# A finer source order, blank matmuls and another load order at the beginning of a fused attention and MoE kernel

## The chip, the cores and the metric

The kernel runs on one core of one Trainium2 chip, as one program. The metric is the device time of that core in microseconds; each run is one execution, and what counts is the median of the runs.

## What is computed

The reference chains three parts. `p` holds 32 pack vectors per head; the attention first packs keys and values into 32 rows per head, and the queries then attend to those rows. The result goes through a mixture of four experts, all of them used, weighted by `domain_probs`, and last through a two-layer map with `h - tanh(h)` between its layers.

```python
q, k, v: (4, 8, 576, 64)   p: (4, 8, 32, 64)      # batch, heads, tokens, head size
def sm_attn(qq, kk, vv):
    s = scale * np.matmul(qq, kk.transpose(0, 1, 3, 2))
    s = s - np.max(s, axis=-1, keepdims=True)
    a = np.exp(s)
    a = a / (np.sum(a, axis=-1, keepdims=True) + 1e-09)
    return np.matmul(a, vv)
p_packed = sm_attn(p, k, v)
out = sm_attn(q, p_packed, p_packed)              # 2304 tokens x 512
for e in range(4):                                # w1: 512 x 1024, w2: 1024 x 512
    h = np.maximum(x @ w1[e], 0.0)
    out += p[:, e:e + 1] * (h @ w2[e])
h = x @ w_in; g = h - np.tanh(h); return g @ w_out
```

## The kernel before

The large products are made of pairs of numbers: a float is split into a high part (`...h`, a copy of 512 to 1024 columns on ScalarE) and a low part (`...l`, the difference on VectorE), and three matmuls stand for one. The tokens are worked in two halves `p` of two batches each, 9 tiles of 128 tokens per half. The experts are worked as 8 chunks `c` of 512 hidden columns.

The program is written as strings of tokens; a letter names a stage, the digits its arguments, and `run` calls them in order.

- **S** `pack_scores`: 4 score matmuls `sc` into a two-bank PSUM tile (pool `ps2`, two such tiles in all, which `tp`, `wps` and `hps` share), `mx` and `nm` on VectorE, the exponential `a` on ScalarE with its sum `ss`, and the norm (`ss`, `rs`, `a`) on VectorE. The digits are the half, then 0 to 3: batch 0 groups 0 and 1, batch 1 groups 0 and 1.
- **T** `pack_T`: five transposes `tp` of `a`, copied out as `a1t` (ScalarE) and `a1e` (VectorE). **P** `pack_pv`: 20 small matmuls `pv` of v with them, copied into `ppbd` by one instruction of ScalarE and one of VectorE.
- **Q** `q_scores`: the q scores `qsc` of two token tiles against `ppbd`, in a one-bank PSUM tile (pool `ps1`, four tiles, which `pv`, `qtp` and `yps` share), and their softmax: `qmx` and the difference on VectorE, the exponential on ScalarE, sum, add, reciprocal and product (`qsm`, `a`) on VectorE. Q04 is one token tile, half as wide. **X** `q_T`: four transposes `qtp`, split into `a2h` and `a2l`.
- **W** `pack_w1`: since x is a2 times packed rows, `ppbd` is multiplied into w1 instead (`wps`, 16 small matmuls, split into `wph` on ScalarE and `wpl` on VectorE). One W per chunk and batch; it needs all of that batch's `P`.
- **u** `up`: the hidden layer of 256 or 320 tokens, 24 matmuls `hps` in two halves, each half in its own `ps2` tile, split into `hu` or `hm`. The last digit is the range of tokens: 0 needs X00, 1 needs X01 and X02 as well and writes the tiles that 2 shares. **d** `down`: 12 matmuls `yps` of one token tile, taken to `x2` by ScalarE in chunk 0, by VectorE later.
- **a** loads half a w1 or w2 chunk; **b** splits w2 (`w2h` on ScalarE, `w2l` on GpSimd in chunk 0, on VectorE later). **K**, **V**, **L** load k, v and q of one batch, in up to four transfers each. **I** and **Z** set up buffers, **n** makes the expert weights from `domain_probs`. `_` is one step of decoding the last map's weights, which goes on in the background.

All loads are issued by SP and share one queue with at most eight in flight. The first ones stand in source order (`manual_schedule` on SP). START_A and START_B, which hold chunk 0 of the experts and all of the attention, are handed to a scheduler that sets the order on each engine from its own estimates; so neighbours in the strings are interleaved there. From chunk 1 on TensorE's order is that of the source. TensorE executes its instructions in order, as every engine does, so a matmul whose operand is late holds all that stand behind it.

Of the kernel before, what the change touches and what calls it, by code (L numbers as in the profile page):

```python
# [8 lines left out]
F32 = mybir.dt.float32  # L9
# [13 lines left out]
R = -11.571460516996891  # L23
# [32 lines left out]
def kernel(  # L56
# [100 lines left out]
    def pack_scores(b, g):  # L157
        sc = ps2.tile([128, 2, 512], F32, tag="p2", name="sc")
        for jj in range(2):
            j = 2 * g + jj  # L160
            for h in range(2):
# [53 lines left out]
    def q_scores(p, t0):  # L215
# [27 lines left out]
        nc.scalar.activation(out=a2[:, 0:n], in_=a2[:, 0:n], func=ACTF.Exp, scale=0.125)  # L243
        sm = small.tile([128, 16, 1], F32, tag="qsm", name="qsm")
# [10 lines left out]
    def q_T(p, t0):  # L255
# [201 lines left out]

    STAGES = {
# [234 lines left out]
```

## Time and profile before

| what | value |
|---|---|
| median of 3 runs (lowest to highest) | 1109.77 us (1108.91 to 1109.89) |
| the profiled execution, its span | 1110.56 us, 1108.8 us |
| TensorE busy | 1090.1 us, 98% of the span, 6420 instructions |
| VectorE busy | 713.5 us, 64%, 967 instructions |
| ScalarE busy | 466.4 us, 42%, 653 instructions |
| GpSimd busy | 7.3 us, 1%, 11 instructions |
| mean granted TensorE clock | 0.996 |
| read and written in HBM | 69.51 MB, 26.21 MB |

The span is what the trace covers, from the first instruction to the last; the 1.76 us that the profiled execution took beyond it lie around it. "Busy" counts the time in which an engine had an instruction under way; matmuls are pipelined, so that it is no measure of TensorE at its peak. In the rows below, an engine's instructions of one kind that follow each other are one row with their count, and the time is that of all of them. Lines are those of the kernel before; `PE` is TensorE, `DVE` VectorE, `ACT` ScalarE, `POOL` GpSimd. What stands behind "<-" is what the idle time ended with: an engine's instruction or a load.

### The profile page before, as it was taken

What the parts mean: (1) busy time and instruction counts of PE and PEld (TensorE: products, weight loads), DVE (VectorE), ACT (ScalarE), POOL (GpSimd) and SP (SyncE); (2) the same over time, 40 slices, a digit from 0 to 9 for tenths busy, and PEclk for the clock granted to TensorE, in tenths of its full rate; (3) what the DMA queues carried; (4) which work ended last, traced back from release to release, by engine and by line L of the source; (5) the groups of instructions that cost most, each with busy time, mean ns of one, the idle gap of its engine ahead of it and who ended that gap; (6) DMA issues with size and microseconds to landing.
All of it is one profiled execution on the core that took longest, in us unless ns stands there. A gap on an engine that the chain in (4) does not pass through costs nothing.

```text
span 1108.8 us, 15316 instructions
## 1 busy us (share of the span) xinstructions
PE 1090.1 (98%) x6420; PEld 911.1 (82%) x6420; DVE 713.5 (64%) x967; ACT 466.4 (42%) x653; POOL 7.3 (1%) x11
## 2 busy tenths in 40 slices
PE   7799999999999999999999999999999999999998
PEld 5587888898888888889888888888888888888887
DVE  4735456766676675676676434487666767777775
ACT  3433433232332332332333112466657656656463
POOL 0100000000000000000000000000000000000000
PEclk9899999999999999999999999999999999999999
DMA  9731013233233241342231042201011262202102
GB/s 332 238 89 39 29 48 115 77 96 114 95 114 95 77 147 63 95 134 77 87 123 58 20 152 77 76 1 38 2 37 39 85 220 95 76 1 76 64 13 76
DMA packets 33668, 96.70 MB, mean 87 GB/s; under 512 B 3776, under 2 KB 3776, under 8 KB 33600
## 3 DMA queue, kind: packets, MB, share of 16 engines
q1 hardware_dynamic: 33600, 95.73, 25.2%
q8 instruction: 50, 0.82, 0.3%
q14 instruction: 18, 0.15, 0.0%
HBM read 69.51 MB, written 26.21 MB: 86 GB/s over the span
## 4 chain that ended last, share of the span: by engine, by line
PE 98%; DVE 1%; ACT 0%; DMA 0%; issue 0%; DVEq 0%; SPq 0%; ACTq 0%
PE yps L391 36%; PE hps L365 18%; PE ops L605 18%; PE h3ps L549 18%; PE wps L340 3%; PE pv L205 1%; PE sc L162 1%; PE qsc L227 1%; PE xps L426 1%; PE qtp L262 1%; PE tp L188 0%; DMA kt<-in_kT_dram 0%; ACT a L173 0%; DVE wpl L347 0%; DVE mx L168 0%
## 5 line engine op out<-in xcount | busy, mean ns | idle before, releaser
L391 PE MATMUL yps<-w2h,hm 128*128 128x512 f32 x640 | 208.4, 394 | 0.0
L549 PE MATMUL h3ps<-xh,ws 128*128 128x512 f32 (+1 forms) x640 | 187.3, 369 | 0.0
L605 PE MATMUL ops<-ws,gh 128*128 128x512 f32 x576 | 178.4, 396 | 0.0
L391 PE MATMUL yps<-w2h,hu 128*128 128x512 f32 x512 | 166.5, 391 | 0.0
L402 DVE SCALAR_TENSOR_TENSOR x<-yps,pn,x 128x512 f32<-128x512 f32 x126 | 94.6, 750 | 100.6 <-PE yps L391 98.0
L365 PE MATMUL hps<-a2h,wph 128*128 128x256 f32 (+1 forms) x512 | 151.8, 297 | 2.4 <-ACT a L173 1.5
L365 PE MATMUL hps<-a2h,wpl 128*128 128x256 f32 (+1 forms) x512 | 151.8, 297 | 0.0
L365 PE MATMUL hps<-a2l,wph 128*128 128x256 f32 (+1 forms) x512 | 151.7, 296 | 0.0
L391 PEld LDWEIGHTS yps<-w2h,hm 128*128 128x128 f32 x640 | 120.1, 188 | 36.3 <-issue 12.6
L549 PEld LDWEIGHTS h3ps<-xh,ws 128*128 128x128 f32 x640 | 116.5, 188 | 20.5
L605 PEld LDWEIGHTS ops<-ws,gh 128*128 128x128 f32 x576 | 107.7, 189 | 24.0 <-ACT gh L584 0.2
L391 PE MATMUL yps<-w2l,hm 128*128 128x512 f32 x320 | 125.2, 391 | 0.0
L549 PE MATMUL h3ps<-xl,ws 128*128 128x512 f32 (+1 forms) x320 | 117.9, 368 | 0.0
L391 PEld LDWEIGHTS yps<-w2h,hu 128*128 128x128 f32 x512 | 96.2, 188 | 19.2
L374 ACT ACTIVATE hu<-hps 128x512 fp32r<-128x512 f32 x64 | 38.2, 598 | 173.1 <-PE hps L365 173.0
L605 PE MATMUL ops<-ws,gl 128*128 128x512 f32 x288 | 110.8, 395 | 0.0
L374 ACT ACTIVATE hm<-hps 128x640 fp32r<-128x640 f32 x64 | 45.1, 704 | 136.1 <-PE hps L365 136.1
L365 PEld LDWEIGHTS hps<-a2h,wph 128*128 128x128 f32 x512 | 97.1, 190 | 6.0 <-ACT a L173 1.7
L391 PE MATMUL yps<-w2l,hu 128*128 128x512 f32 x256 | 100.1, 391 | 0.0
L365 PEld LDWEIGHTS hps<-a2l,wph 128*128 128x128 f32 x512 | 97.2, 190 | 2.3
L365 PEld LDWEIGHTS hps<-a2h,wpl 128*128 128x128 f32 x512 | 97.1, 190 | 0.5 <-issue 0.4
L375 DVE SCALAR_TENSOR_TENSOR hm<-hps,hm 128x640 fp32r<-128x640 f32 x64 | 52.7, 823 | 61.1 <-ACT hm L374 61.1
(90 smaller groups left out, 1392.1 us busy)
## 6 DMA issues: line engine op xcount, KB each, us to landing
w1f<-in_w_dram SPq DMA_DIRECT2D x16, 512.0 KB, 4.9
st<-in_w_dram SPq DMA_DIRECT2D x16, 512.0 KB, 3.8
f<-in_win_dram SPq DMA_DIRECT2D x16, 512.0 KB, 3.5
f<-in_wout_dram SPq DMA_DIRECT2D x16, 512.0 KB, 3.5
win<-fo SPq DMA_DIRECT2D x16, 512.0 KB, 2.6
wout<-fo SPq DMA_DIRECT2D x16, 512.0 KB, 2.6
ws<-win SPq DMA_DIRECT2D x16, 512.0 KB, 4.6
ws<-wout SPq DMA_DIRECT2D x16, 512.0 KB, 4.7
```

Of the source, the lines that this page charges most:

```text
L162: nc.tensor.matmul(out=sc[64 * jj:64 * jj + 64, h, 0:288], lhsT=pbd[:, 4 * b + j, :], rhs=kv_k[b][j][:, 288 * h:288 * h + 288],)
L205: nc.tensor.matmul(out=pv[64 * h:64 * h + 64, jj, :], lhsT=kv_v[b][c][0:n, 128 * j + 64 * h:128 * j + 64 * h + 64], rhs=a1t[:, c, k0:k0 + ...
L227: nc.tensor.matmul(out=sc[r - r0:r - r0 + 64, 256 * i:256 * i + 256].rearrange("p (r j k) -> p r j k", r=2, j=4)[:, :, j, :], lhsT=qs[2 * ...
L262: nc.tensor.transpose(tp[:, g, i, :], a2[:, c0:c0 + 128], ident)
L340: nc.tensor.matmul(out=ps[32 * j:32 * j + 32, r, :], lhsT=ppbd[p][d, bi, j, 32 * r:32 * r + 32], rhs=w1f[c, j // 2][d, j % 2, :],)
L365: nc.tensor.matmul(out=ps[:, ff, 0:n], lhsT=a[c, p, bi][:, g, c0:c0 + 128], rhs=x[p][:, g, t0:t0 + n], start=(k == 0), stop=(k == 5),)
L374: last[1] = nc.scalar.activation(out=hi[:, :, d], in_=ps[:, :, 0:n], func=ACTF.Relu).ins
L375: last[0] = nc.vector.scalar_tensor_tensor(out=lo[:, :, d], in0=ps[:, :, 0:n], scalar=0.0, in1=f(hi[:, :, d]), op0=ALU.max, op1=ALU.subtra ...
L391: nc.tensor.matmul(out=ps, lhsT=a[:, ff, o:o + 128], rhs=w[c, fp][:, ff], start=(k == 0), stop=(k == 11),)
L402: last[0] = nc.vector.scalar_tensor_tensor(out=x2[tt], in0=ps, scalar=pn[:, tt, e:e + 1], in1=x2[tt], op0=ALU.mult, op1=ALU.add,).ins
L549: nc.tensor.matmul(out=ps[:, ff, 0:n], lhsT=w[:, wl, kd, :], rhs=x[:, kd, :], start=(k == 0), stop=(k == 11),)
L605: nc.tensor.matmul(out=ops[u][t], lhsT=a[ff][:, d], rhs=w[:, wl], start=(i == 0 and ff == 0 and k == 0), stop=(i == 3 and ff == 1 and k == 2),
```

## The change

Five things change, all of them in the attention and chunk 0.

1. S is cut into M (matmuls), E (max and exponential) and N (norm), and Q's norm becomes R, so that the source can put other work between. S stays as the three in a row.
2. T takes two one-bank tiles of `ps1` (`tp`, `te`) in place of one two-bank tile of `ps2`, and `a1e` is copied by ScalarE.
3. `fill` issues blank matmuls: 128x128, float, of a tile of zeros with itself, into a `ps1` tile `warm` that nothing reads. There are 26: 7 at the start, 5 before T00, 5 before M02, 5 before X00 and 4 before T02. While it lives, three `ps1` tiles are left for the rest.
4. TensorE, SP, VectorE and ScalarE follow the source in START_A and START_M, SP also in START_L, and TensorE to the end of the experts. In between, VectorE and ScalarE are the scheduler's from START_L on. The first `up` (u000) stands before M03, T03, P03, W001 and Q02, and the steps d000 and d001 before u001. `q_T` records its last instructions in `last`, and the expert weights (n) are issued after `last[0]`.
5. The first loads come as pst, k0, v0, domain_probs, q0, k1, w1 (2), v1, w2 (2), q1; before it was pst, k0, k1, v0, v1, w1 (2), domain_probs, q0, q1, w2 (2). Chunk 1's first pair of w2 loads (a110, a111), which SP issued after V3 and from 50.08 us on, now stands ahead of K2, K3, V2 and V3 there. Batch 1's tiles come from the pools of the later ones; `p_att` has 12 buffers in place of 18.

```diff
-START_A = (
-    "S00 S01 S02 T00 S03 T01 P00 T02 P01 T03 P02 P03 Z0 a100 a101 "
-)
+START_A = "f7 M00 E00 M01 E01 N00 N01 f5 T00 T01 P00 P01 Q00 Q01 f5 M02 f5 R00 E02 N02 X00 "
+
+START_M = "W000 f4 T02 R01 u000 b00 M03 X01 E03 P02 b01 N03 T03 P03 W001 Q02 "
+
+START_L = "R02 K2 I1 n K3 V2 V3 d000 Q04 R04 Q03 R03 d001 X02 S10 S11 "
 
 START_B = (
-    "W000 Q00 Q01 X00 K2 W001 I1 n Q02 X01 S10 u000 V2 b00 b01 K3 V3 X02 S11 Q04 Q03 u001 d000 X03 S12 "
-    "T10 u002 S13 X04 d001 T11 d002 P10 d003 T12 P11 P12 T13 L2 u003 d005 d004 P13 L3 Z1 Q10 Q11 W010 "
-    "W011 d006 Q12 X10 d007 d008 u010 a010 Q13 X11 d010 X12 a011 u011 Q14 X13 d011 u012 a110 "
+    "u001 X04 X03 d002 T10 S12 u002 S13 T11 P10 d003 T12 P11 d004 T13 P12 L2 u003 d005 P13 L3 Z1 d006 Q10 R10 "
+    "Q11 R11 W010 W011 d007 Q12 R12 X10 d008 u010 a010 Q13 R13 X11 d010 X12 a011 u011 Q14 R14 X13 d011 u012 a110 "
     "X14 d013 u013 a111 b10 d012 W100 d015 W101 d016 d014 d017 b11 d018 u100 "
 )
...
-    def pack_scores(b, g):
-        sc = ps2.tile([128, 2, 512], F32, tag="p2", name="sc")
+    scs, sms = {}, {}
+
+    def pack_mm(b, g):
+        sc = scs[b, g] = ps2.tile([128, 2, 512], F32, tag="p2", name="sc")
...
+
+    def pack_exp(b, g):
+        sc = scs.pop((b, g))
...
+        a1s[b, g] = a1, ss
+
+    def pack_norm(b, g):
+        a1, ss = a1s[b, g]
         nc.vector.tensor_scalar(out=ss, in0=ss, scalar1=1e-9, scalar2=None, op0=ALU.add)
         rs = small.tile([128, 1], F32, tag="rs", name="rs")
         nc.vector.reciprocal(out=rs, in_=ss)
         nc.vector.tensor_scalar(out=a1, in0=a1, scalar1=rs, scalar2=None, op0=ALU.mult)
         a1s[b, g] = a1
 
+    def pack_scores(b, g):
+        pack_mm(b, g)
+        pack_exp(b, g)
+        pack_norm(b, g)
+
     def pack_T(b, g):
         a1 = a1s.pop((b, g))
-        tp = ps2.tile([128, 2, 4, 128], F32, tag="p2", name="tp")
-        for c in range(5):
-            n = 128 if c < 4 else 64
-            nc.tensor.transpose(tp[0:n, c // 4, c % 4, :], a1[:, 128 * c:128 * c + n], ident)
+        tp = ps1.tile([128, 4, 128], F32, tag="p1", name="tp")
+        te = ps1.tile([128, 128], F32, tag="p1", name="te")
+        for c in range(4):
+            nc.tensor.transpose(tp[:, c, :], a1[:, 128 * c:128 * c + 128], ident)
+        nc.tensor.transpose(te[0:64, :], a1[:, 512:576], ident)
         a1t = att_tile(b, [128, 4, 128], "a1t")
         a1e = att_tile(b, [128, 128], "a1e")
-        nc.scalar.activation(out=a1t, in_=tp[:, 0], func=ACTF.Copy)
-        nc.vector.tensor_copy(out=a1e[0:64], in_=tp[0:64, 1, 0])
+        nc.scalar.activation(out=a1t, in_=tp, func=ACTF.Copy)
+        nc.scalar.activation(out=a1e[0:64], in_=te[0:64], func=ACTF.Copy)
...
+        a2s[p, t0] = a2, a23, G
+
+    def q_norm(p, t0):
+        a2, a23, G = a2s[p, t0]
...
-        nc.scalar.activation(out=a2h[p][:, :, d], in_=src, func=ACTF.Copy)
-        nc.vector.tensor_tensor(
+        last[1] = nc.scalar.activation(out=a2h[p][:, :, d], in_=src, func=ACTF.Copy).ins
+        last[0] = nc.vector.tensor_tensor(
             out=a2l[p][:, :, d], in0=src, in1=f(a2h[p][:, :, d]), op=ALU.subtract
-        )
+        ).ins
...
+    def fill(n):
+        for i in range(n):
+            nc.tensor.matmul(out=warm[:, i % 4, :], lhsT=blank, rhs=blank)
+
+    def late_norm():
+        with tc.issue_after(last[0]):
+            norm_probs()
...
+    blank = const.tile([128, 128], F32, name="blank")
+    nc.vector.memset(blank, 0.0)
+    warm = ps1.tile([128, 4, 128], F32, tag="p1", name="warm")
     pst = p_att.tile([128, 4 * B, 32], F32, tag="a", name="pst")
     with tc.manual_schedule(engines={mybir.EngineType.SP}):
         nc.sync.dma_start(out=pst, in_=pT)
         load_k(0)
+        load_v(0)
+        nc.sync.dma_start(out=pn, in_=dp)
+        load_q(0)
         load_k(1)
-        load_v(0)
-        load_v(1)
         stage(0, 0, 0)
         stage(0, 0, 1)
-        nc.sync.dma_start(out=pn, in_=dp)
-        load_q(0)
+        load_v(1)
+        stage(1, 0, 0)
+        stage(1, 0, 1)
         load_q(1)
...
-    run(START_A)
+    rest = {mybir.EngineType.SP, mybir.EngineType.DVE, mybir.EngineType.Activation}
+    pe_order = ExitStack()
+    pe_order.enter_context(tc.manual_schedule(engines={mybir.EngineType.PE}))
+    begin = ExitStack()
+    begin.enter_context(tc.manual_schedule(engines=rest))
+    run("Z0 " + START_A)
     att_stack.close()
     p_wp = pool("wp", 2, pa)
+    p_hm = pool("hm", 4, pa)
     p_hu = pool("hu", 8, pa)
-    p_hm = pool("hm", 4, pa)
-    p_w2 = pool("w2", 8, pa)
+    run(START_M)
+    begin.close()
+    with tc.manual_schedule(engines={mybir.EngineType.SP}):
+        run(START_L)
     run(START_B)
-    with tc.manual_schedule(engines={mybir.EngineType.PE}):
-        for c in range(1, NCH):
-            w = {"c": c, "e": c + 1}
-            nxt = c + 1 < NCH
-            run(EVEN % w)
-            run(ODD % w if nxt else LAST)
+    for c in range(1, NCH):
+        w = {"c": c, "e": c + 1}
+        nxt = c + 1 < NCH
+        run(EVEN % w)
+        run(ODD % w if nxt else LAST)
+    pe_order.close()
```

What this does to the engines' order shows at three places. In the rows below, each engine's instructions stand in order; an xN counts neighbours of a kind, a number behind `a_` tells buffers apart, and what stands left of "<-" is written.

TensorE in after, from M03 (`sc`) over X01, P02, T03 (`tp`, `te`), P03, W001 and Q02 to d000:

```order
L166 MATMUL sc<-kt,pbd 64x288 x4
L283 MATMUL qtp<-ident,a_384 128x128 x4
L222 MATMUL pv<-a1t,vt 64x32 x8
L222 MATMUL pv<-a1e,vt 64x32 x2
L222 MATMUL pv<-a1t,vt 64x32 x8
L204 MATMUL tp<-ident,a_522 128x128 x4
L205 MATMUL te<-ident,a_522 64x128
L361 MATMUL wps<-w1f,ppbd 32x512 x8
L244 MATMUL qsc<-ppbd,qt 64x2x32 x16
L412 MATMUL yps<-w2h,hu 128x512
```

TensorE in before, from the `wps` of W000 over P02, P03, the rest of W000, Q00 with Q01, W001, X00, Q02 and X01 to the first `up`:

```order
L340 MATMUL wps<-w1f,ppbd 32x512 x2
L205 MATMUL pv<-a1t,vt 64x32 x8
L205 MATMUL pv<-a1e,vt 64x32 x2
L340 MATMUL wps<-w1f,ppbd 32x512 x6
L227 MATMUL qsc<-ppbd,qt 64x2x32 x32
L340 MATMUL wps<-w1f,ppbd 32x512 x8
L262 MATMUL qtp<-ident,a_462 128x128 x4
L227 MATMUL qsc<-ppbd,qt 64x2x32 x16
L262 MATMUL qtp<-ident,a_489 128x128 x4
L162 MATMUL sc<-kt,pbd 64x288 x2
L365 MATMUL hps<-a2h,wph 128x256
```

What moved: W000's and W001's `wps` stood ahead of X00 and around Q00; W001 now stands behind P03, the transposes of T03 between P02 and P03, and the first `up` ahead of all these rows, with the blanks.

TensorE in after, from the end of d001 over X02, S10 and S11 to the first half of u001:

```order
L412 MATMUL yps<-w2l,hu 128x512
L412 MATMUL yps<-w2h,hu 128x512
L283 MATMUL qtp<-ident,a_622 128x128 x4
L166 MATMUL sc<-kt,pbd 64x288 x8
L386 MATMUL hps<-a2h,wph 128x320
L386 MATMUL hps<-a2l,wph 128x320
L386 MATMUL hps<-a2h,wpl 128x320
```

TensorE in before at u001, from the end of u000 over the second half of S11, X02 and Q04 with Q03, with the first `yps` of d000 after the first matmul of u001:

```order
L365 MATMUL hps<-a2h,wpl 128x256
L162 MATMUL sc<-kt,pbd 64x288 x4
L262 MATMUL qtp<-ident,a_551 128x128 x4
L227 MATMUL qsc<-ppbd,qt 64x2x32 x24
L365 MATMUL hps<-a2h,wph 128x320
L391 MATMUL yps<-w2h,hu 128x512
L365 MATMUL hps<-a2l,wph 128x320
L365 MATMUL hps<-a2h,wpl 128x320
```

What moved: d000 and d001, and both scores, now stand whole ahead of u001, where d000 stood among its matmuls.

VectorE in after, the norms of Q04 (`a_694`) and Q03 (`a_721`), then X02's `a2l` and the maxima of S10 and S11:

```order
L257 TENSOR_TENSOR a_721<-qsc,qmx 128x512
L266 TENSOR_REDUCE qsm<-a_694 128x8
L267 TENSOR_SCALAR qsm<-qsm 128x8
L270 RECIPROCAL qsm<-qsm 128x8
L266 TENSOR_REDUCE qsm<-a_721 128x16
L271 TENSOR_TENSOR a_694<-a_694,qsm 128x256
L267 TENSOR_SCALAR qsm<-qsm 128x16
L270 RECIPROCAL qsm<-qsm 128x16
L287 TENSOR_TENSOR a2l<-qtp,a2h 128x2x256
L271 TENSOR_TENSOR a_721<-a_721,qsm 128x512
L175 TENSOR_REDUCE mx<-sc 128x1 x2
L177 TENSOR_SCALAR nm<-mx 128x1 x2
```

VectorE in before, the same kind of work of Q02 (`a_551`) up to its product:

```order
L266 TENSOR_TENSOR a2l<-qtp,a2h 128x2x256
L245 TENSOR_REDUCE qsm<-a_551 128x16
L168 TENSOR_REDUCE mx<-sc 128x1
L246 TENSOR_SCALAR qsm<-qsm 128x16
L170 TENSOR_SCALAR nm<-mx 128x1
L249 RECIPROCAL qsm<-qsm 128x16
L375 SCALAR_TENSOR_TENSOR hu<-hps,hu 128x512
L250 TENSOR_TENSOR a_551<-a_551,qsm 128x512
```

What moved: the steps of one softmax were set between those of others and of u000 (`hu`) and S10 (`mx`); now two softmaxes come whole ahead of the two maxima.

## Rows read from the trace of the kernel before

**Rows 1.** TensorE's waits: line, <- releaser: us in total, times, longest us.
```profile
PE qtp L262 <- DVE qsm L246: 5.4, 1, 5.4
PE sc L162 <- DMA kt<-in_kT_dram: 4.3, 1, 4.3
...
PE hps L365 <- ACT a L173: 1.5, 1, 1.5
```

**Rows 2.** Timeline, TensorE: start us, us, engine, line, operation, tiles, xcount [idle before <-releaser].
```profile
4.35 5.24 PE L162 MATMUL sc<-kt,pbd 128*64 128x288 f32 x16 [4.35 <-DMA kt<-in_kT_dram]
10.58 1.20 PE L162 MATMUL sc<-kt,pbd 128*64 128x288 f32 x8 [0.99 <-ACT a L173]
11.80 0.74 PE L188 MATMUL tp<-ident,a 128*128 128x128 f32 x5
...
17.77 0.66 PE L205 MATMUL pv<-a1t,vt 128*64 128x32 f32 x16
...
25.40 2.13 PE L227 MATMUL qsc<-ppbd,qt 128*64 128x64 f32 x64
27.46 1.09 PE L340 MATMUL wps<-w1f,ppbd 64*32 64x512 f32 x16
33.90 1.09 PE L262 MATMUL qtp<-ident,a 128*128 128x128 f32 x4 [5.36 <-DVE qsm L246]
...
49.20 0.42 PE L365 MATMUL hps<-a2h,wph 128*128 128x320 f32 x1
```

**Rows 3.** Windows: us, five engines' busy us (instructions), TensorE's granted clock, DMA share, GB/s.
```profile
32.00:33.00 1.00, 0.00 (x0) 0.00 (x0) 1.00 (x3) 0.00 (x0) 0.00 (x0) 0.66 1.08 395
39.00:40.00 1.00, 1.00 (x5) 0.42 (x4) 0.91 (x2) 0.57 (x2) 0.00 (x0) 0.93 1.12 347
```

**Rows 4.** Chain that ended last, 150 to 160 us: start us, us, what.
```profile
152.89 5.46 PE yps L391 x24
```

**Rows 5.** Groups, 0 to 140 us, VectorE: tiles, xcount | busy, mean ns | idle before.
```profile
L347 DVE TENSOR_TENSOR wpl<-wps,wph 128x1024 fp32r<-128x1024 f32 x6 | 7.2, 1212 | 4.4 <-ACT wph L346 4.4
...
L168 DVE TENSOR_REDUCE mx<-sc 128x1 f32<-128x576 f32 x8 | 6.1, 756 | 8.5 <-PE sc L162 8.5
...
L250 DVE TENSOR_TENSOR a<-a,qsm 128x512 f32<-128x512 f32 x8 | 5.5, 684 | 0.1
...
L237 DVE TENSOR_REDUCE qmx<-qsc 128x16 f32<-128x512 f32 x8 | 5.4, 683 | 1.7 <-PE qsc L227 1.7
...
L249 DVE RECIPROCAL qsm<-qsm 128x16 f32<-128x16 f32 x8 | 2.0, 246 | 0.1
...
L246 DVE TENSOR_SCALAR qsm<-qsm 128x16 f32<-128x16 f32 x8 | 1.3, 166 | 0.1
...
L250 DVE TENSOR_TENSOR a<-a,qsm 128x256 f32<-128x256 f32 x2 | 0.8, 416 | 0.0
```

**Rows 6.** The same groups, 0 to 140 us, ScalarE.
```profile
L173 ACT ACTIVATE a<-sc,nm 128x576 f32<-128x576 f32 x8 | 5.9, 738 | 9.5 <-DVE nm L170 6.4 <-PE tp L188 1.9 <-DVE rs L179 1.2
L346 ACT ACTIVATE wph<-wps 128x1024 fp32r<-128x1024 f32 x6 | 5.9, 1016 | 1.2 <-PE wps L340 1.2
...
L265 ACT ACTIVATE a2h<-qtp 128x512 fp32r<-128x512 f32 x8 | 4.8, 597 | 10.8 <-PE qtp L262 10.8
...
L173 ACT ACTIVATION_READ_ACCUMULATOR a<-sc,nm 128x1 f32 x8 | 1.6, 196 | 0.0
```

**Rows 7.** Timeline, GpSimd's row of 40 to 60 us, then VectorE's of 51 to 52.5.
```profile
47.67 4.74 POOL L114 TENSOR_TENSOR w2l<-st,w2h 128x1024 fp32r<-128x1024 f32 x2 [44.58 <-ACT w2h L113]
...
51.37 1.07 DVE L246 TENSOR_SCALAR qsm<-qsm 128x8 f32<-128x8 f32 x1
52.35 0.51 DVE L180 TENSOR_SCALAR a<-a,rs 128x576 f32<-128x576 f32 x1
```

**Rows 8.** Timeline, TensorE, ahead of the `up` at 111.38.
```profile
109.53 0.38 PE L262 MATMUL qtp<-ident,a 128*128 128x128 f32 x2
...
111.38 0.56 PE L365 MATMUL hps<-a2h,wph 128*128 128x320 f32 x2
```

More of the change, by code (lines that the diff above doesn't have):

```diff
@@ L95 @@
     ps1 = pool("ps1", 4, space=PSUM)
+    p_w2 = pool("w2", 8, pa)
     att_stack = ExitStack()
-    p_att = pool("att", 18, att_stack)
+    p_att = pool("att", 12, att_stack)
     def u2t(shape, dt, name):
@@ L120, in att_tile @@
     def att_tile(b, shape, name):
-        if b < 2:
+        if b < 1:
             return p_att.tile(shape, F32, tag="a", name=name)
@@ L138, in load_v @@
             if n == 2:
-                pl, tg = (p_att, "v2") if b < 2 else (p_w2, "w2")
-                t = pl.tile([128, 2, 512], F32, tag=tg, name="vt", **({"bufs": 4} if b < 2 else {}))
+                pl, tg = (p_att, "v2") if b < 1 else (p_w2, "w2")
+                t = pl.tile([128, 2, 512], F32, tag=tg, name="vt", **({"bufs": 2} if b < 1 else {}))
                 nc.sync.dma_start(
@@ L456, in background @@
             next(bg, None)
+    def fill(n):
[4 more added lines that the diff above has]
+            norm_probs()
     STAGES = {
         "S": lambda p, i: pack_scores(2 * p + i // 2, i % 2),
+        "M": lambda p, i: pack_mm(2 * p + i // 2, i % 2),
+        "E": lambda p, i: pack_exp(2 * p + i // 2, i % 2),
+        "N": lambda p, i: pack_norm(2 * p + i // 2, i % 2),
+        "R": lambda p, i: q_norm(p, 2 * i),
         "T": lambda p, i: pack_T(2 * p + i // 2, i % 2),
@@ L468 @@
         "L": load_q,
-        "n": norm_probs,
+        "n": late_norm,
+        "f": fill,
         "a": stage,
```

## The prediction

> **What bounds the kernel now.** I read the page's first two parts, then TensorE's waits, then the timeline of the first 50 us, and last the groups of VectorE and ScalarE. TensorE is busy 98% of the span, so the time can only fall by what it waits, or by what a slow clock stretches. The list of waits over the whole span is short: 5.4 us once for VectorE's norm of the first q scores, 4.3 us for the first load, 1.5 us for an exponential [rows 1]; what is left is smaller. These three lie in the first 46 us. Behind the 5.4 us lies a second loss: TensorE went idle 5.36 us before 33.90, so at 28.54 [rows 2]. The granted clock averaged 0.66 between 32 and 33 us and 0.93 between 39 and 40 [rows 3]. As there are two levels, 2.4 GHz (1) and 1.2 (one half), that puts the fall at 32.32 and the return at 39.14. So the clock fell 3.8 us after the pause began, and stayed at half for 5.25 us after work began again at 33.90, which costs about 2.6 us. The pause of 1.5 us did not cost the clock. What the beginning can give back, the first load left alone, is therefore the 5.4, the 1.5, the smaller waits and the 2.6.
>
> **How the sum is made.** At 49.20 before begins its second `up` (u001) [rows 2]. In after, all that TensorE did ahead of that point is done ahead of its u001 too, and in addition the two `down` steps d000 and d001: 24 yps matmuls, 5.46 us by a row of that count [rows 4]. So order alone leaves the time where it is if u001 begins at 49.20 + 5.46 = 54.7 us. I follow the chain to that matmul, then add the clock and what lies behind.
>
> **From the first load to the first q scores.** The first loads are the same two k tiles, so the first pack score waits for the same data. Before it ran 16 score matmuls in 5.24 us [rows 2], against 1.20 for 8 later on [rows 2]; part is data, part is slow steps. With f7 ahead of it I take M00 to end at 7.6 and the first `mx` to begin at 7.7. Then mx 0.76 [rows 5], exp 0.74 + 0.20 [rows 6], ss, rs and the product, 0.5 [rows 7], and small ones put T00 at 11.1, against 11.80 [rows 2]. Then a1t, a copy of 512 columns as a2h is, 0.60 [rows 6], and P00 and P01. A half of P takes 0.66 for its first 16 matmuls [rows 2] and a quarter of that for its last 4, so a P is 1.65. They run from 12.6 to 15.8. `a1e` moves from VectorE to ScalarE, where it stands behind a1t: between 0 and a second 0.6, I take 0.3, hidden by the 16 pv matmuls that need only a1t. Q00 is half of the 2.13 that 64 qsc matmuls take [rows 2], so VectorE begins qmx at about 17.6. That is the real gain: W000 no longer stands ahead of the q scores.
>
> **From there to u000.** VectorE now has, in source order: qmx and sub of Q00 and Q01 (0.68 each), R00 (sum and product 0.68 each, add 0.17, reciprocal 0.25), M02's mx (0.76) and nm, a wait for the exponential (0.94), its norm (0.51 for the product, 0.3 for two small ones), a2l (0.68, as the others of 512 columns) and wpl (1.21) [rows 5 to 7]. That is 9.1 and fills 17.6 to 26.8. u000's first half is 12 matmuls, some 1.6 us, and two steps that empty its buffer, 0.60 on ScalarE and 0.69 on VectorE; at 29.6 that two-bank buffer is free for M03. M03 takes 1.2, then comes a chain through three engines: ScalarE is still with hu, w2h and a2h (0.60); VectorE with a2l, mx and nm; then exp 0.94, ppbd's copies behind it, and the norm, 0.83 [rows 5 to 7]. T03 can start at 36.3. TensorE has X01 and P02 for that time and has done P02 by 33.0: a **first pause** of 3.3 us.
>
> **From there to u001.** T03 0.74, a1t and a1e 0.9, P03 1.65, 0.5 for its small copies, W001's 16 matmuls 1.09 [rows 2] and wph 1.02 [rows 6] bring VectorE's wpl to 42.3. Behind it in source order stand, before u001's buffer is free: nine instructions of 512 columns (0.68), four of 256 (0.42), three pairs of add and reciprocal (0.17 and 0.25), two mx (0.76) and one nm [rows 5]. With wpl that is 1.2 + 6.1 + 1.7 + 1.3 + 1.5 = 11.8, and 0.7 of waiting for an exp that nothing covers. Neighbours that don't depend on each other overlap by 0.09, as 52.35 begins before 51.37 + 1.07 [rows 7]; that takes 0.6 off. So the last nm is done at about 54.2, the exp 0.94 later, and u001 begins at **55.2**. TensorE meanwhile has W001, Q02, d000, Q04, Q03, d001, X02 and both scores: done at 51.9, a **second pause** of 3.3 us. Against 54.7 the order gives **+0.5 us**. The second half of u001 waits for the buffer of the other score: **+0.4**.
>
> **Further back.** X12's four transposes stand directly ahead of u011, which reads what they make. Before they are two and two among yps: 0.38 at 109.53 is the last pair, and u011 begins at 111.38 with no idle [rows 8]. In after the last pair of transposes (0.38), a2h 0.60 and a2l 0.68 (like its neighbours of 512 columns) [rows 5, 6] stand between the last yps and u011, 1.66 us, of which I take 0.2 as covered: **+1.5** (bounds 0, if other work covers it, and 2).
>
> **The blanks** are 128x128 on zeros, a shape that the trace has only as transposes (5 in 0.74 [rows 2], 0.11 a step). I take double a step, 0.22 (bounds 0.11 and 0.45 at half clock). f7 ends before the first k tile; f5, f5, f5 and f4 end 0.4 to 1.0 us ahead of T00, M02, X00 and T02. They cost nothing, and take one of ps1's four buffers only until the last.
>
> **The loads.** 288 KB at the 395 GB/s of [rows 3] is 0.75 us, 512 KB 1.3. v0 lands at 11 to 12 (needed 12.6), q0 at 15.1 (15.8), k1 at 18 (19.5), w1 at 20.7 (22.8): covered, by half a microsecond at the tightest. On SP chunk 1's pair of w2 loads, whose buffer is free when GpSimd is done at about 38, now stands ahead of K2, K3, V2 and V3; kt then lands by 46 and S10 asks at 50. Cost nothing; 4 us of cover.
>
> **The clock.** Two pauses of 3.3 us lie between one that kept the clock (1.5) and one that lost it 3.8 us in [rows 1, 3]. The nearer row is the 3.8, but neither pause reaches it; the work around them is thin (pv, qsc, transposes). I take one fall, **+2.5**, bounds 0 and 5.2.
>
> **The sum.** 0.5 + 0.4 + 1.5 + 2.5 = +4.9 us. The profiled execution took 1110.56 (span 1108.8 and 1.76 around it), so after's own would take 1115.4; the median of the runs stands 0.79 lower, which gives **1114.5**.
>
> **The rivals.**
> Both pauses lose the clock: +7.4, 1117.1. For it: the shape of before's loss. Against: each is short of 3.8 us.
> Neither does: +2.4, 1112.1, on the edge of what a measurement of this kernel can tell from no change (0.2%, 2.2 us).
> VectorE meets GpSimd: the second w2l on GpSimd covers the time at which N03's product stands in VectorE's queue (35 to 36 us). Before shows such a meeting: the add at 51.37 took 1.07, ending with GpSimd's 47.67 + 4.74 = 52.41 [rows 7], where its like is 0.17 [rows 5]. One w2l is 2.4 us, so up to +2.1 on the chain, 1116.6. It decides if the product starts after the w2l has; my margin is 0.4 us. The Trainium skill ("SBUF — State Buffer", section "Who interferes with whom") says of such pairs that whoever issues first holds the shared ports for its whole instruction and the other is blocked; this speaks against source order on VectorE, which can't put another instruction there. The row agrees: the add ends as GpSimd does. By that rule the sum is +7.0 if the product comes second, and +4.9 if it doesn't.
> The blanks don't do what they are for: if matmuls on zeros raise or hold nothing, M00 runs at half speed and the early pauses count too: +1 to +3 more, 1115.5 to 1118.
> The other side: the chain of VectorE is shorter. I put three exponentials (0.94), a2h and wph in series with VectorE's queue, some 4.5 us. If VectorE finds queued work under them, both pauses go, the clock stays, and u001 begins when TensorE is free, at 51 or before: −3.7 + 0.5 behind, 1106.6. It decides from u001 at 52 on. For it: before's VectorE did fill such gaps. Against: that was with an order its scheduler chose; source order fills none.
>
> **How the numbers follow.** One fall 0.30, both 0.12, none 0.24, the meeting 0.07, idle blanks 0.06, the shorter chain 0.21. "None" stands on the bound of 1112.0 and is split, 0.12 and 0.12; of the shorter chain 0.18 is faster than 1107.6 and 0.03 is not. Slower: 0.30 + 0.12 + 0.07 + 0.06 + 0.12 = 0.67; same 0.15; faster 0.18. The range, 1107 to 1118, takes in all of the first five and the upper half of the shorter chain, and leaves out what goes well past the prices named, about 0.1 at either end.
>
> **What would show it.** TensorE's waits: one on T03 for VectorE's product (3.3 us, about 33 to 36), one on u001's hps for an exp (about 52 to 55), one on u011's hps for a2l (near 117). u001 at 55.2 is right, at 51 the shorter chain. The granted clock from 33 to 62 us says which of the first three cases holds; qsc of Q00 near 16 us with T00 at 11.1 shows the first legs. Wrong would be a wait on a load (K2's S10, or q0), which I costed at nothing, or u001 later than 58.

## The result, and the profile after

The changed kernel takes 1117.03 us in the median, before 1109.80: slower by 0.64%, ratio 1.0064 with a 95% interval of 1.0044 to 1.0083, or 7.2 us (4.9 to 9.2). One execution of the four, disturbed at 3354 us, counts in that median; the other three lie between 1115.95 and 1117.31, with 1116.76 in the middle. The forecast was 1114.5 in 1107 to 1118, slower with 0.67. The profiled execution took 1116.76, with a span of 1114.9: 6.2 us more than the one of before.

Part 1 of the page, each engine's busy time, answers to the table of before:

```profile
PE 1099.9 (99%) x6472; PEld 919.4 (82%) x6472; DVE 711.5 (64%) x960; ACT 468.6 (42%) x661; POOL 7.2 (1%) x11
```

TensorE is busy for 9.8 us more and idle for 3.7 less. Nearly all of the 3.7 is the wait for the first load: blanks now fill it, and TensorE first waits 1.05 us where it was 4.35 [rows 2]. So behind the first load the pauses have moved rather than shrunk; what is busy on top is blanks and the same work at half clock. TensorE's waits (line, <- releaser: us in total, times, longest us), which answer to [rows 1]:

```profile
PE tp L204 <- DVE a L191: 3.1, 2, 2.9
PE hps L386 <- ACT a L180: 2.3, 1, 2.3
...
PE hps L386 <- ACT a2h L286: 0.8, 1, 0.8
...
PE hps L386 <- DVE a2l L287: 0.3, 1, 0.3
```

The 5.4 us on a q score's norm are gone. In their place stand 2.9 on T03 (`tp`, for the product of N03), 2.3 on u001 (for the exponential of S10) and 0.8 + 0.3 on u011: the three places that the prediction named. TensorE's timeline (start, us, engine, line, operation, tiles, count, idle before), which answers to [rows 2]:

```profile
4.33 4.15 PE L166 MATMUL sc<-kt,pbd 128*64 128x288 f32 x16
...
10.51 0.63 PE L204 MATMUL tp<-ident,a 128*128 128x128 f32 x4 [0.71 <-ACT a L180]
...
16.09 1.85 PE L244 MATMUL qsc<-ppbd,qt 128*64 128x64 f32 x56 [0.20 <-DVE ppbd L230]
...
35.27 1.09 PE L204 MATMUL tp<-ident,a 128*128 128x128 f32 x4 [2.87 <-DVE a L191]
...
39.75 2.57 PE L361 MATMUL wps<-w1f,ppbd 64*32 64x512 f32 x16
42.26 2.46 PE L244 MATMUL qsc<-ppbd,qt 128*64 128x64 f32 x32
...
52.56 2.21 PE L166 MATMUL sc<-kt,pbd 128*64 128x288 f32 x16
57.09 0.41 PE L386 MATMUL hps<-a2h,wph 128*128 128x320 f32 x1 [2.32 <-ACT a L180]
```

The rows are, in order: M00 and M01, T00, most of Q00 and Q01, T03, W001, Q02, S10 with S11, u001. W001 takes 2.57 where the same 16 matmuls took 1.09 in [rows 2], Q02 2.46 for half of what took 2.13: the clock. Windows of the granted clock (us, five engines' busy us, clock, DMA share, GB/s), which answer to [rows 3]:

```profile
32.00:36.00 4.00, 1.13 (x14) 1.01 (x11) 2.69 (x11) 1.88 (x4) 2.04 (x2) 0.81 0.46 122
36.00:44.00 8.00, 7.53 (x86) 4.88 (x86) 0.73 (x2) 1.99 (x4) 1.33 (x1) 0.50 0.69 226
44.00:48.00 4.00, 4.00 (x35) 3.11 (x33) 3.17 (x6) 0.84 (x2) 0.00 (x0) 0.91 0.97 344
56.00:60.00 4.00, 2.91 (x15) 2.91 (x16) 1.83 (x9) 1.92 (x5) 0.00 (x0) 0.80 0.01 2
60.00:64.00 4.00, 4.00 (x22) 3.82 (x21) 1.65 (x3) 1.81 (x4) 0.00 (x0) 0.77 0.00 0
```

The level is one half (1.2 GHz) from 34.48 (0.81 over four us is 1.52 us of half clock) to 44.72, and again from 58.40 to 61.84. The first of these fell 2.1 us into the pause ahead of T03 and lasted until 9.4 us after work began again; the second fell 1.3 us after u001 had begun, behind the second pause. VectorE's timeline shows what it did meanwhile:

```profile
7.55 0.76 DVE L175 TENSOR_REDUCE mx<-sc 128x1 f32<-128x576 f32 x1 [3.60 <-PE sc L166]
...
17.05 0.69 DVE L254 TENSOR_REDUCE qmx<-qsc 128x16 f32<-128x512 f32 x1 [1.02 <-PE qsc L244]
...
24.84 1.21 DVE L368 TENSOR_TENSOR wpl<-wps,wph 128x1024 fp32r<-128x1024 f32 x1
...
34.60 0.52 DVE L191 TENSOR_SCALAR a<-a,rs 128x576 f32<-128x576 f32 x1
40.12 0.23 DVE L230 COPY ppbd<-pv 64x64 f32<-64x64 f32 x1 [5.00 <-ACT ppbd L229]
43.50 1.22 DVE L368 TENSOR_TENSOR wpl<-wps,wph 128x1024 fp32r<-128x1024 f32 x1 [3.15 <-ACT wph L367]
```

The rows are M00's maximum, Q00's, W000's `wpl`, the product of N03, P03's copy and W001's `wpl`. Between 35.12 and 43.50 VectorE does one instruction of 0.23 us: it waits for TensorE's T03, P03 and W001, which run at half clock, while the work that it will be short of time for stands behind `wpl`.

The ledger, against u001 at 54.66 (49.20 and 5.46): u001 at 57.09 is +2.4; the second half clock, 3.44 us, costs 1.7 by an estimate (half of its length); u011 waits 1.1. That is 5.3 of the 6.2 us. The other 0.9 come in between 65 and 165 us, where no further wait is listed; they were not traced to a place, and their cause stays open.

### The profile page after: what moved, and what is told of

It reads as the page before. It is cut to its first block, busy times and chain, and to the rows that moved or that the text cites. A ratio compares the mean times of both kernels' runs of the same rounds, so it can differ in the third digit from the quotient of the medians.

```text
span 1114.9 us, 15419 instructions
## 1 busy us (share of the span) xinstructions
PE 1099.9 (99%) x6472; PEld 919.4 (82%) x6472; DVE 711.5 (64%) x960; ACT 468.6 (42%) x661; POOL 7.2 (1%) x11
## 4 chain that ended last, share of the span: by engine, by line
PE 96%; DVE 1%; DMA 1%; ACT 1%; issue 0%; DVEq 0%; ACTq 0%
PE yps L412 35%; PE hps L386 18%; PE ops L652 18%; PE h3ps L596 18%; PE wps L361 3%; PE pv L222 1%; DMA vt<-in_v_dram 1%; PE qsc L244 1%; PE xps L447 1%; PE sc L166 1%; PE tp L204 0%; ACT a L180 0%; PE warm L481 0%; PE qtp L283 0%; DVE mx L175 0%
## 5 line engine op out<-in xcount | busy, mean ns | idle before, releaser
L652 PEld LDWEIGHTS ops<-ws,gh 128*128 128x128 f32 x576 | 107.5, 189 | 24.1 <-ACT gh L631 0.2
```

The lines of the kernel that those rows point to most:

```text
L652: nc.tensor.matmul(out=ops[u][t], lhsT=a[ff][:, d], rhs=w[:, wl], start=(i == 0 and ff == 0 and k == 0), stop=(i == 3 and ff == 1 and k == 2),
```

## Experiments

Each is timed beside the kernel before, and its ratio and interval are to that; times are medians. "The changed kernel" is the one of the diff in "The change".

### Blanks away

```diff
-START_A = "f7 M00 E00 M01 E01 N00 N01 f5 T00 T01 P00 P01 Q00 Q01 f5 M02 f5 R00 E02 N02 X00 "
+START_A = "M00 E00 M01 E01 N00 N01 T00 T01 P00 P01 Q00 Q01 M02 R00 E02 N02 X00 "
-START_M = "W000 f4 T02 R01 ...
+START_M = "W000 T02 R01 ...
```

> The changed kernel without its 26 blank matmuls; all else as it is. Theory A (the blanks raise the clock before the first score and hold it in the waits ahead of T00, M02, X00 and T02): M00's first maximum begins near 8.6 instead of 7.55, the clock falls somewhere between 8 and 25 us, and the time is 1118 to 1120. Rival (matmuls on zeros do nothing for the clock, the early pauses are too short to matter): 1117.0, with the first maximum at 7.55.

Measured: 1121.73 (ratio 1.0108, 1.0093 to 1.0123), 4.7 us above the changed kernel and 1.7 above what theory A allowed. M00 with M01 on TensorE, and M00's maximum on VectorE:

```profile
4.41 5.97 PE L166 MATMUL sc<-kt,pbd 128*64 128x288 f32 x16 [4.41 <-DMA kt<-in_kT_dram]
8.50 0.76 DVE L175 TENSOR_REDUCE mx<-sc 128x1 f32<-128x576 f32 x1 [4.50 <-PE sc L166]
```

and the windows, with the changed kernel's own 12 to 28 as the last row:

```profile
12.00:28.00 16.00, 13.31 (x174) 10.85 (x182) 6.76 (x16) 3.79 (x11) 0.00 (x0) 0.67 1.04 378
28.00:32.00 4.00, 3.17 (x24) 1.41 (x9) 2.83 (x6) 2.80 (x6) 0.00 (x0) 0.63 0.46 178
12.00:28.00 16.00, 15.08 (x225) 12.14 (x224) 9.93 (x21) 5.83 (x13) 0.00 (x0) 1.00 1.04 383
```

The maximum begins at 8.50, not 7.55, and from 12 to 28 us the clock is half for two thirds of the time where the changed kernel holds it at 1. The first scores show the raise: M00 and M01 take 5.97 here and 4.15 in the changed kernel, and over all profiles 5.16 to 5.97 without blanks ahead of them and 4.15 to 5.02 with seven. So matmuls on zeros do raise and hold the clock, and the rival of the prediction in which they don't falls. Its price, +1 to +3, was too low: the half clock lasted from 13.9 to 24.1 us, and for 3 of the 4 us from 28 to 32.

### Blanks in the first pause

```diff
-... P02 b01 N03 T03 P03 W001 Q02 "
+... P02 b01 N03 f9 T03 P03 W001 Q02 "
```

> The changed kernel with nine more blanks (about 2.5 us) between P02 and T03, where TensorE waits 2.87 us for VectorE. Theory A (the half clock from 34.5 to 44.7 stands on the chain T03, P03, W001, wpl, VectorE's queue, u001): the clock stays at 1, wpl begins at 40.6 instead of 43.50, u001 at 54.2 instead of 57.09, the time falls by 2.9 to 1114.1; the pause ahead of u001 grows to nearly 4. Rival (VectorE's queue is held by something else, so u001 stays where it is): the clock stays at 1, the pause ahead of u001 grows to 5, and the time is 1116.5 to 1117.5.

Measured: 1114.22 (1.0036, 1.0025 to 1.0047). Theory A, by the time and by the place of u001; TensorE at T03, W001 and u001, and the windows:

```profile
35.68 0.63 PE L204 MATMUL tp<-ident,a 128*128 128x128 f32 x4 [0.67 <-DVE a L191]
...
38.64 1.71 PE L361 MATMUL wps<-w1f,ppbd 64*32 64x512 f32 x16
...
54.53 0.61 PE L386 MATMUL hps<-a2h,wph 128*128 128x320 f32 x1 [2.80 <-ACT a L180]
```

```profile
36.00:44.00 8.00, 7.42 (x102) 5.35 (x101) 2.67 (x4) 2.00 (x4) 1.74 (x1) 1.00 0.67 225
52.00:60.00 8.00, 5.47 (x27) 5.46 (x28) 5.01 (x17) 2.36 (x6) 0.00 (x0) 0.79 0.27 90
```

The clock stays at 1 from 36 to 44, W001 takes 1.71 with its wait for P03's copy in it, and u001 begins at 54.53: 2.56 earlier, though T03 itself comes 0.41 later. This is the price of the first half clock on the path, but not all of it is clock: W001's `wpl` comes 1.98 earlier (41.52 against 43.50), and the other 0.6 come behind it, where VectorE's order is the scheduler's (it was set free from START_L on) and differs between the two kernels. The order alone puts u001 at 54.53 against the 54.66 of before, so the order's own term is −0.1. The pause ahead of u001 grew to 2.80, not to 4, and the clock still falls behind it (0.79 over eight us, 3.4 us of half clock).

That second fall does not come in every execution. Each execution's mean granted clock was recorded with its time, and one fall of 3.4 us makes it 0.998. Of the seven of this kernel, two have 1.000 and took 1112.17 and 1112.35; three, the profiled one among them, have 0.998 and took 1113.65 to 1114.42; the other two have 0.996 and 0.995, and took 1114.78 and 1116.50. So one such fall costs some 1.3 to 2.3 us, which takes in the 1.7 of the ledger, and the same kernel lost the clock in some executions and kept it in others (only the one was traced).

### Blanks in both pauses

The nine blanks ahead of T03, and

```diff
-... d001 X02 S10 S11 "
+... d001 X02 S10 S11 f8 "
```

> As the kernel with nine blanks ahead of T03, and eight more blanks between S11 and u001. Theory A: neither pause costs the clock; against the kernel with blanks at T03 alone the half clock of 58.4 to 61.8 goes, 1.7 us: 1112.4. Rival (the second fall comes from thin work before the pause, or from elsewhere): 1114, and the half clock behind u001's start is still there.

Measured: 1114.46 (1.0043, 1.0028 to 1.0058); neither theory's account. The half clock behind u001 is gone, but two things take its place. A wait that the others don't have:

```profile
PE yps L412 <- DVE a L257: 1.8, 1, 1.8
```

The blanks' tile keeps one of ps1's four buffers until the last blank, and d001 waits for VectorE's last reading of a q score, so for the buffer that frees. And the clock:

```profile
36.00:40.00 4.00, 3.42 (x55) 2.29 (x56) 0.23 (x1) 0.97 (x3) 1.45 (x1) 0.73 0.40 97
40.00:44.00 4.00, 4.00 (x50) 2.57 (x39) 1.61 (x2) 1.03 (x1) 0.00 (x0) 0.84 0.97 360
```

It is at half for 3.4 us between 36 and 44, after the same work that kept it in the run with the first blanks alone. Up to there the two kernels issue the same instructions; only the execution differs. u001 begins at 56.34. The one execution of the four with a mean clock of 1.000 took 1113.35, about 1.1 more than the like ones of the run before: so without a fall in either kernel the eight blanks cost about that much.

### Q04 and Q03 behind u001

```diff
-START_L = "R02 K2 I1 n K3 V2 V3 d000 Q04 R04 Q03 R03 d001 X02 S10 S11 "
+START_L = "R02 K2 I1 n K3 V2 V3 d000 d001 X02 S10 S11 "
-    "u001 X04 X03 d002 ...
+    "u001 Q04 R04 Q03 R03 X04 X03 d002 ...
```

> The changed kernel with Q04, R04, Q03, R03 moved behind u001, so 4.9 us of VectorE's work no longer stand between wpl and u001. Theory A (VectorE's queue in source order sets u001): the pause ahead of u001 goes, u001 begins near 53 instead of 57.09, with 1.6 us of q scores done later; no second fall of the clock; the time falls by 2.3 + 1.7 to 1113. Rival (the chain over S10's exponential is what is late, whatever stands ahead of it): u001 at 56 to 57, 1116 to 1117.

Measured: 1121.43 (1.0099, 1.0083 to 1.0116): far from both. TensorE at u001, X04 and X03:

```profile
55.63 0.41 PE L386 MATMUL hps<-a2h,wph 128*128 128x320 f32 x1 [1.43 <-ACT a L180]
...
64.01 0.66 PE L283 MATMUL qtp<-ident,a 128*128 128x128 f32 x2 [3.04 <-DVE a L271]
66.29 1.08 PE L283 MATMUL qtp<-ident,a 128*128 128x128 f32 x4 [1.62 <-DVE a L271]
```

u001 came 1.5 us earlier, though T03 was 1.0 later in this execution, and waits 1.43, so VectorE's queue ahead of it mattered. But the q softmaxes, 4.9 us of VectorE, then stood between u001 and the two transposes X04 and X03, with nothing on TensorE to cover them: 3.04 and 1.62 of waits, and a half clock from 63 to 70. The work was moved past one wait into another. The expectation had counted 1.6 us of q scores behind u001 and nothing for the softmaxes that X04 and X03 wait for.

### X12 ahead of d010

The blanks ahead of T03, and

```diff
-... Q13 R13 X11 d010 X12 a011 u011 ...
+... Q13 R13 X11 X12 d010 a011 u011 ...
```

> The changed kernel with the nine blanks ahead of T03 (as in the run of that alone, 1114.2) and X12 moved ahead of d010, so that u011 no longer reads what the transposes directly ahead of it make. Theory A: the waits of 0.83 and 0.31 at u011 go and nothing takes their place: 1113.1. Rival (the wait is VectorE's queue, not the place of X12, and comes back at u011 or d010): 1114.2.

Measured: 1112.91 (1.0027, 1.0017 to 1.0037), 1.3 below the run without it, and the two waits at u011 are off the list. In the changed kernel they read

```profile
114.39 0.60 PE L283 MATMUL qtp<-ident,a 128*128 128x128 f32 x4
115.82 0.41 PE L386 MATMUL hps<-a2h,wph 128*128 128x320 f32 x1 [0.83 <-ACT a2h L286]
116.54 0.41 PE L386 MATMUL hps<-a2l,wph 128*128 128x320 f32 x1 [0.31 <-DVE a2l L287]
```

which is the transposes, then the wait for `a2h` and the wait for `a2l`: 1.14 where the prediction had 1.5.

### Independent work in the pauses

```diff
-START_M = "W000 f4 ... b01 N03 T03 P03 W001 Q02 "
+START_M = "K2 W000 f4 ... b01 N03 M10 f7 T03 E10 P03 N10 W001 Q02 M11 E11 "
-START_L = "R02 K2 I1 n K3 V2 V3 d000 Q04 R04 Q03 R03 d001 X02 S10 S11 "
+START_L = "R02 N11 I1 n K3 V2 V3 d000 Q04 Q03 X02 R04 R03 d001 "
```

with X12 ahead of d010 as well.

> The changed kernel with independent work where the engines wait: K2's loads at the head of START_M, S10's scores and seven blanks in the pause ahead of T03, its exponential behind T03, S11's scores and maximum behind Q02, X02 ahead of d001, and X12 ahead of d010. Theory A (VectorE idles from 35.1 to 43.5 while T03, P03 and W001 run, and its queue behind wpl sets u001): S10's and S11's maxima leave the queue behind wpl, u001 begins near 53.3 instead of 57.09, no half clock ahead of it or behind it; with 1.7 for the second fall and 1.1 for u011 that is 6.7 off 1117.0: 1110.3. Rival (the clock falls in the thin work of 36 to 44 us whatever fills the pause): 2 to 3 us more, 1112 to 1113.

Measured: 1110.15 (1.0000, 0.9991 to 1.0010): the same time as before, as expected to 0.2 us, though not quite for the reasons given. Both pauses are gone, but a wait of 1.4 on d001 is new, for the buffer that X02 holds until `a2l` is made, and the clock is at half from 50.2 to 53.6:

```profile
PE yps L412 <- DVE a2l L287: 1.4, 1, 1.4
```

```profile
48.00:52.00 4.00, 2.59 (x9) 1.88 (x8) 3.52 (x9) 2.22 (x4) 0.00 (x0) 0.78 0.81 267
52.00:56.00 4.00, 4.00 (x20) 3.52 (x19) 1.41 (x5) 0.69 (x1) 0.00 (x0) 0.80 0.02 7
```

### The same with Q03 behind X02, twice

```diff
-START_L = "R02 N11 I1 n K3 V2 V3 d000 Q04 Q03 X02 R04 R03 d001 "
+START_L = "R02 N11 I1 n K3 V2 V3 Q04 d000 d001 X02 Q03 R04 R03 "
-    "u001 X04 X03 d002 T10 S12 u002 ...
+    "u001 X04 T10 S12 X03 d002 u002 ...
```

> The kernel of S10's scores in the pause (1110.2) with Q04 ahead of d000, d001 ahead of X02, Q03 behind X02, and behind u001 X04, T10, S12, X03, d002 in this order. There the trace showed 1.41 us in which d001 waited for X02's low part, and the granted clock at half from about 50.2 to 53.6. Theory A (a short pause after thin work costs the clock, and filling it keeps it): the wait of 1.41 and the half clock (1.7) go, 1107.0. Rival (the clock falls after the thin work of 36 to 48 us even without a pause): the half clock moves and stays, 1108.5 to 1109.

> The same kernel as the one with Q03 behind X02, a second time, to see whether the half clock from 16.6 to 20 us, with no pause ahead of it, belongs to the kernel or to the execution. Theory A (a fall in thin work comes in some executions and not in others): this profile shows none there, or one elsewhere, and the times spread over the same 1107.6 to 1108.7. Rival (it belongs to the kernel's order): the same 3.4 us of half clock at the same place, 1108.3.

Measured: 1108.31 (0.9984, 0.9975 to 0.9993) and, the second time, 1107.93 (0.9985, 0.9975 to 0.9994): faster than before by 1.6 and 1.9 us. The windows of 16 to 20 us, of the first profile and of the second:

```profile
16.00:20.00 4.00, 3.80 (x63) 3.63 (x61) 2.03 (x4) 0.63 (x1) 0.00 (x0) 0.57 1.03 397
```

```profile
16.00:20.00 4.00, 3.80 (x76) 3.34 (x74) 2.91 (x6) 0.63 (x1) 0.00 (x0) 1.00 1.03 396
```

In the first the clock is at half for 3.4 us of the window, from 16.2 to 19.6, in the midst of the q scores, with no wait of TensorE above 0.2 us in the 4.5 us ahead; in the second, of the same kernel, it isn't. So this fall belongs to the execution. The mean clocks say the same of more than two: of the kernel's 21 executions five have 0.998, as the first profile, and 1108.57 in the median; twelve have 1.000, as the second, and 1107.95. With the wait of 1.4 on d001, in the run before this, seven of ten had 0.998. In the second profile the granted clock reads 1 up to the last microseconds, and u001 begins at

```profile
50.07 0.41 PE L386 MATMUL hps<-a2h,wph 128*128 128x320 f32 x1
```

that is 4.6 us before the 54.66 of the ledger. The span is 3.3 us shorter than before's, so 1.3 of it are lost again behind u001; 0.77 of them are two new waits there (0.54 for X03's norm, 0.23 for a buffer of S12).

### Three blanks among the thin work

```diff
-... T00 T01 P00 P01 Q00 Q01 ...
+... T00 T01 P00 f1 P01 f2 Q00 Q01 ...
```

in the kernel just told of.

> The same kernel with one more blank between P00 and P01 and two between P01 and Q00, in the thin work of 12 to 16 us. Theory A (the fall at 16.6 comes from the pv and qsc work and blanks among it prevent it): no half clock from 16 to 20, minus 1.7, and some 0.5 later through Q00: 1107.1. Rival (three blanks are too few, or the fall is chance): 1108.5 to 1109.

Measured: 1107.76 (0.9982, 0.9973 to 0.9991), with no half clock in the first 200 us of its profile; two of its ten executions have a mean clock of 0.998. Against 1107.93 and 1108.31 that is no difference to speak of; whether the blanks prevented a fall stays open, since the kernel without them has profiles of both sorts.

### VectorE and ScalarE left to the scheduler

```diff
-    rest = {mybir.EngineType.SP, mybir.EngineType.DVE, mybir.EngineType.Activation}
+    rest = {mybir.EngineType.SP}
```

> The changed kernel with VectorE and ScalarE left to the scheduler in START_A and START_M; TensorE and SP as in the change. It puts Q01's norm ahead of M02's maximum and of a2l and wpl. Theory A (source order on VectorE is worth something there: X00 and T02 come first): T02 and u000 start 2.5 us later, T03 and u001 about 1.4 later: 1118 to 1119. Rival (source order is what makes the pauses, and the scheduler fills them): T03's pause shrinks below 2 us and u001 comes earlier, 1115.

Measured: 1122.03 (1.0111, 1.0096 to 1.0127), 5 us above the changed kernel: theory A by its direction, but 3 us past what it allowed. TensorE's waits for the products of the pack norms:

```profile
PE tp L204 <- DVE a L191: 7.0, 4, 4.2
```

In the changed kernel they were 3.1 in all, the longest 2.9. The scheduler sets Q01's norm ahead of M02's maximum and of `wpl`; T02 waits 1.80 for it and T03 then 4.22. At T03 something else has a part, the meeting with GpSimd that the prediction had as a rival. The first row is GpSimd's two `w2l`, the others are two of VectorE's steps for the expert weights (n), which stand ahead of N03's product in its queue:

```profile
33.62 4.66 POOL L116 TENSOR_TENSOR w2l<-st,w2h 128x1024 fp32r<-128x1024 f32 x2 [30.53 <-ACT w2h L115]
35.25 0.77 DVE L461 TENSOR_SCALAR psum<-psum 128x18 f32<-128x18 f32 x1
36.35 2.02 DVE L463 TENSOR_TENSOR pn<-pn,psum 128x72 f32<-128x72 f32 x1
```

In the changed kernel they take 0.17 and 0.23, the first as a `w2l` ends and the second between the two; here the first ends 0.05 us behind the first `w2l` and the second 0.1 behind the second. That is 2.4 us ahead of N03's product. So the rival falls, since neither pause shrinks; but how much of the 5 us is the order of the norms and how much is the meeting that this order brings was not separated.

### The kernel before, with blanks in its one long pause

```diff
-    "W000 Q00 Q01 X00 K2 W001 I1 n Q02 ...
+    "W000 Q00 Q01 W001 f9 f8 X00 K2 I1 n Q02 ...
```

and `fill`, `blank` and `warm` as in the change.

> The kernel before with seventeen blanks behind W001, in its 5.36 us wait ahead of X00, and nothing else. Theory A (the pause cost 2.6 us of half clock on TensorE's path, and blanks hold the clock): no half clock from 32 to 39 us, 1107.2. Rival (the chain over VectorE sets the end of that stretch, so a slower clock there was hidden): 1109.8, with the clock at 1.

Measured: 1107.58 (0.9979, 0.9969 to 0.9988), 2.2 us faster than before, of the 2.6 that the prediction had read from the half clock. TensorE's blanks, X00 and u001's first matmul, and the windows that were 0.66 and 0.93 at their ends in [rows 3]:

```profile
28.30 4.06 PE L460 MATMUL warm<-blank 128*128 128x128 f32 x34
33.73 0.63 PE L262 MATMUL qtp<-ident,a 128*128 128x128 f32 x4 [1.36 <-DVE qsm L246]
...
46.40 0.41 PE L365 MATMUL hps<-a2h,wph 128*128 128x320 f32 x1
```

```profile
32.00:36.00 4.00, 2.64 (x43) 2.24 (x42) 3.54 (x9) 0.60 (x1) 0.00 (x0) 1.00 1.07 364
36.00:40.00 4.00, 4.00 (x23) 2.49 (x21) 2.60 (x5) 1.83 (x3) 0.00 (x0) 1.00 1.05 306
```

The pause has shrunk from 5.36 to 1.36 behind the blanks, the clock is at 1, and u001 begins at 46.40 instead of 49.20. Of these 2.80 us X00 has 0.17 already (33.73 against 33.90), so 2.6 come behind the pause: the price of the half clock, as read.

## Why the prediction was right, and where its sizes were off

- **The first legs** held: M00's maximum at 7.55 (7.7 forecast), T00 at 10.51 (11.1), Q00's maximum at 17.05 (17.6), W000's `wpl` done at 26.05 (26.8). The chain was a little faster than summed, by 0.2 at its beginning and 0.6 to 0.8 from T00 on.
- **The first pause** came where it was put, for the instruction named: T03 at 35.27 after 2.87 us (36.3 after 3.3).
- **u001** was forecast at 55.2 with the clock at 1 up to there. With the clock held, it begins at 54.53, so the order's term is −0.1 and not +0.5; the 0.4 for u001's second half did not appear, as no wait stands there. The 0.6 by which the first legs were early is most of it. One reason given for this wait does not hold: the prediction has VectorE behind W001's `wpl` in source order, which "fills none". By the change itself its order is the scheduler's from START_L on, and the rows of VectorE in "The change" show it: both maxima (`mx`) come ahead of both `nm`, so S10's exponential waits for S11's maximum too. The sum counts both maxima and so is right in this; a source order there was not tried.
- **The clock** is the term that was mis-sized. One fall was taken, at 2.5; the first costs 2.6 on u001 and 2.8 in the time, near what was taken. But both pauses brought one: the second costs 1.7. The rival "both pauses lose the clock", given 0.12, is what happened. That its 1117.1 stands so near 1117.03 is in part luck: with its terms as measured (−0.1, 0, 1.1, 2.6 and 1.7) its +7.4 is +5.3, and 0.9 that no term names bring this to the 6.2 between the profiles. (The forecast's own total is off by 0.2 as well: 1109.77 + 4.9 is 1114.7.) The step that failed is the argument against it, that each pause is shorter than the 3.8 us of [rows 1, 3]: the first fall came 2.1 us into its pause, the second only after it. One observed delay was read as a bound; and as the mean clocks of the run with blanks ahead of T03 show, one kernel loses the clock in some executions and not in others, so that no single row could give one.
- **u011** costs 1.14 (1.5 forecast); the run that moves X12 gains 1.3.
- **GpSimd's meeting** did not happen: the product of N03 ran from 34.60 for its usual 0.52, and GpSimd's second `w2l` began 0.36 us into it:

```profile
34.96 2.36 POOL L116 TENSOR_TENSOR w2l<-st,w2h 128x1024 fp32r<-128x1024 f32 x1 [1.96 <-ACT w2h L115]
```

  It took its usual time too (2.36; 4.74 for two in [rows 7]), though the two overlap by 0.16. The margin was 0.36 us (0.4 forecast). VectorE came first, which is the order in which the rule of the Trainium skill ("SBUF — State Buffer", section "Who interferes with whom") has GpSimd wait; no stretch of these rows shows GpSimd stretched by it. The other order, GpSimd first, came in the run with the scheduler's order on VectorE, and cost 2.4 us: the rival's price, for other instructions than the one it named.
- **The shorter chain**, the forecast's other side, did not come of itself: VectorE did not find work under T03, P03 and W001, and idled there for 8 us. When S10's and S11's maxima were put there and the waits that this brought were filled too, it came: u001 at 50.07, against the 51 that the rival had worked out, and 1107.9 against its 1106.6.
- **The loads** were covered, as forecast: none is in the list of waits.

What the change gained by its earlier q scores it lost again because it pulled u000 far ahead of what makes u001 ready. With the clock held (the run with blanks ahead of T03) u000 ends at 29.4 and u001 begins at 54.5: 25.1 us, of which TensorE waits 4.0 and does blanks for 2.3, so it has 18.8 us of work to stand there against a chain of 25.1 that passes through VectorE several times (M03's maximum and norm, P03's copy, `wpl` and the queue behind it). That this is the cause is shown by the runs that filled the gap: blanks ahead of T03 give back 2.8 of the 7.2 us, and with independent work (and seven blanks) in the pauses and X12 moved it is 6.9. The share of the second pause alone was not isolated by a run, since the blanks there brought a wait of their own; its 1.7 rests on the estimate and on the recorded clocks of single executions. The 0.9 behind u001 has no cause shown.

## What to carry to other kernels

When a matmul block is pulled forward, sum the vector work that its successor needs against the matmul work left to stand between them; if the former is longer, the pause has only moved. Price every pause of a few us of the tensor engine twice, once as idle time and once as the half clock that may follow it, even where it is shorter than the one that lost the clock before. And before a rewrite, fill the one long pause with blank matmuls: here these few lines gave 2.2 us, at least as much as the whole rewrite with its flaws mended (1.6 and 1.9). And look at the granted clock of every execution, not of the profiled one alone, before a short fall is put down to the kernel.

## What the runs showed of the hardware

- Blank matmuls on zeros, whose result nothing reads, hold the granted clock: without 26 of them the changed kernel is 4.7 us slower.
- The clock fell in or behind pauses of 2.87, 2.32 and 2.80 us; in one profile it fell behind a wait of 1.4 us, and in one with no wait of TensorE above 0.2 us in the 4.5 us ahead of it. The Trainium skill ("TensorE: Matmul & The Clock Gate", section "HAM oscillation — how this bites in real kernels") lays such falls to gaps in TensorE's work; the last of these has none to speak of.
- The same instructions up to 36 us kept the clock until 44 in one kernel's profile and lost 3.4 us to half clock in another's; two profiles of one kernel differed in the same way from 16 us on. A single profile does not tell whether a short fall belongs to the kernel; the mean clocks of its executions do (0.998 in 5 of 21, 1.000 in 12).
- VectorE steps that met a GpSimd `w2l` under way took 0.77 and 2.02 us instead of 0.17 and 0.23, and ended 0.05 and 0.1 us behind it.
